# Attention feeding a two-layer FFN on one core: new costs in the planner, and x, softmax sums and gated activations that stay in PSUM

## The chip, the cores and the metric

The program runs on one core of a Trainium2 chip, in one launch. The metric is the device time of that launch in microseconds (us). Three runs of the kernel before took 990.47, 990.62 and 991.66 us; the median, 990.62 us, is the number to compare with. One more execution was recorded by the profiler. Its own device time was 991.34 us, and the stretch from its first to its last instruction, the span, was 989.3 us.

## The reference

For 8 batches of 8 heads (576 positions, 64 columns per head) two attentions are added: one over q, k and v averaged in groups of 4 positions, its output repeated 4 times, and one over a band of 7 positions around each position. The sum, seen as 4608 tokens of 512 columns, goes through two matrix products with a gate between them.

```python
q_d = q.reshape(B, H, Sd, 4, D).mean(axis=3)          # also k_d, v_d
out_d = softmax_attention(q_d, k_d, v_d)              # scale 1/sqrt(64)
out_up = np.repeat(out_d, 4, axis=2)
mask = np.abs(pos[:, None] - pos[None, :]) < 4
out_local = masked_softmax_attention(q, k, v, mask)
x = (out_up + out_local)  # -> [4608, 512]

h = x @ w_in                                          # [4608, 2048]
g = where(h >= 1, h, where(h <= -1, 0, (h + 1)**2 / 4))
return g @ w_out                                      # [4608, 512]
```

All inputs are float32, and q and k are drawn eight times larger than v.

## The kernel before

**Products.** TensorE multiplies in a reduced format (fp32r), so the big products are made from three: each matrix is split into a high part and a low part, and high times high, high times low and low times high are summed in PSUM. That is why x exists as `xh` and `xl`, the gate's output as `gh` and `gl`, and each weight block as two halves.

**The FFN.** The tokens are cut into chunks of 512, 256 and then ten of 384. For each chunk and each of 16 blocks of 128 hidden columns, `mm1` makes h in one PSUM bank with 12 matmuls (L647), four engine steps gate it (ScalarE relu and square at L659 and L660, VectorE minimum at L661, ScalarE cast to `gh` at L663, GpSimd subtraction to `gl` at L668), and `mm2` adds the block's part of the output into up to four PSUM banks (L687). Two banks take turns for h. The weights come as raw 64-bit words and are converted on the chip in chunk 0 (`convert`: two ScalarE steps at L608 and L610, VectorE at L613 and L615, ScalarE at L620, VectorE at L623); after that they stay in SBUF.

**Attention.** It works on pairs of heads, four pairs to a batch, 32 in all. A pair passes these steps: VectorE sums q and k over groups of 4 (`qd`, `kd`, L340 and L344); TensorE makes the band scores in ten windows (L358, L370) and the pooled scores (L395); VectorE and ScalarE make maxima, exponentials and sums (L418 to L472); TensorE transposes both sets of weights (L488, L504), ScalarE copies them out (`al` L494, `ap` L512); GpSimd adds v over groups of 4 (`vh` L478, `vd` L480); TensorE multiplies with v (L527) and with vd (L545); ScalarE scales the pooled result (`xd` L555), VectorE adds both (`x` L563), ScalarE casts it to `xh` (L577) and GpSimd subtracts to get `xl` (L582). Batch 0 is needed before chunk 0 can start; later pairs are worked in between the FFN's matmuls, each a chunk ahead. x lives in a ring that holds two batches.

**What sets the order.** Every step is first recorded as an operation with an engine, a cost, what it needs, the buffers it holds, and a key. `Plan.run` then simulates five engines with these costs, always takes the operation that can start earliest (within a window of 0.15 us the lowest key wins), and so fixes each engine's order and each buffer's place. The program is then written out in that order. Each engine works its list strictly in order on the chip, so an operation that waits holds up everything behind it on its engine, wherever the chip's times differ from the plan's. Loads and stores are all issued from SyncE's queue, in the planned order too. PSUM has eight banks; a pair's PSUM tiles take two neighbouring ones, during batch 0 any of four such places, later only banks 0 and 1 (with bank 2 for part of the scores).

Of the kernel before, what the change touches and what calls it, by code (L numbers as in the profile page):

```python
# [17 lines left out]
P = 128  # L18
# [56 lines left out]
class Op:  # L75
    __slots__ = ("eng", "cost", "fn", "deps", "bufs", "key", "n", "left", "next", "start", "end", "nbytes", "name", "shared")


class Plan:
# [4 lines left out]
    DMA_RATE = 370e3  # L84
    DMA_LATENCY = 2.0
    WINDOW = 0.15
    BACKLOG = 4.0

    def __init__(self):
        self.ops = []  # L90
        self.pools = {}
# [4 lines left out]
    def op(self, eng, cost, fn, deps=(), bufs=(), key=0.0, nbytes=0, name="", shared=False):  # L96
        o = Op()
        o.eng, o.cost, o.fn, o.key, o.n = eng, cost, fn, key, len(self.ops)
        o.deps = list({id(d): d for d in deps if d is not None}.values())
        o.bufs, o.nbytes, o.name, o.shared = list(bufs), nbytes, name, shared  # L100
        for b in o.bufs:
            b.users += 1
        self.ops.append(o)
        return o

    def run(self):
# [9 lines left out]
        avail = {}  # L116
        busy = set()
        users = {}
        dma_free = 0.0
        pool_busy = []  # L120
        for o in self.ops:
            if not o.left:
                ready[o.eng].append(o)

        def settle(o):
            t = 0.0
            for d in o.deps:
                e = d.end
                if d.eng != o.eng:
                    e += self.PE_LATENCY if d.eng == "PE" else self.LATENCY  # L130
                t = max(t, e)
            return t
# [11 lines left out]
        based = {}  # L144
        done = []
        total = len(self.ops)
        while len(done) < total:
            best = None
            for e in engines:
                cands = []  # L150
                for o in ready[e]:
                    t = based.get(o.n)
                    if t is None:
                        t = based[o.n] = settle(o)
                    ok = True
                    for b in o.bufs:
                        if b.units is None:
                            got = pick(b)
                            if got is None:
                                ok = False  # L160
                                break
                            t = max(t, got[0] + self.LATENCY)
                    if ok:
                        if e == "SP":
                            t = max(t, dma_free - self.BACKLOG)
                        cands.append((max(t, free[e]), o))
                if not cands:
                    continue
                t0 = min(c[0] for c in cands)
# [595 lines left out]
```

## Time and profile before

| | before |
|---|---|
| median of 3 runs | 990.62 us (990.47 to 991.66) |
| profiled execution, its own time | 991.34 us |
| its span | 989.3 us |
| TensorE busy | 964.3 us, 97% of the span |
| VectorE busy | 431.8 us, 44% |
| ScalarE busy | 487.4 us, 49% |
| GpSimd busy | 340.1 us, 34% |
| first matmul of the FFN starts | 49.99 us |

In the profile PE is TensorE's matmuls, PEld its weight loads, DVE VectorE, ACT ScalarE, POOL GpSimd, and SPq SyncE's queue, which issues the loads and stores. Times in a trace are us from the span's start, a duration in a group's row is ns. A row of a timeline has the start, the duration, the engine, the line, the operation, the tiles (written<-read) with their shapes, how many were merged, and in brackets how long the engine had been idle before and what ended that wait. Consecutive instructions on one engine overlap a little: a row's duration runs to the acknowledged end, and the next one may start some 0.08 us earlier.

### The profile page before, as it was taken

How to read it: one execution, taken by the hardware profiler on the slowest of the kernel's cores; microseconds unless marked ns; L12 is line 12 of the kernel's file. 1: busy time of each engine (PE TensorE's matmuls, PEld its weight loads, DVE VectorE, ACT ScalarE, POOL GpSimd, SP SyncE). 2: the span in 40 equal slices, each digit the busy share in tenths (PEclk: the TensorE clock that was granted, in tenths of full speed). 3: DMA queues.
4: the chain of work that ended last, by engine and by line, in shares of the span. 5: the costliest groups of instructions: out<-in, count | busy, mean ns of one | idle time of the engine just before them, and what ended most of it. 6: DMA issues, size and time to landing. Idle time of an engine off the chain costs nothing.

```text
span 989.3 us, 18499 instructions
## 1 busy us (share of the span) xinstructions
PE 964.3 (97%) x7620; PEld 835.6 (84%) x7620; DVE 431.8 (44%) x704; ACT 487.4 (49%) x1063; POOL 340.1 (34%) x320
## 2 busy tenths in 40 slices
PE   6699999999999999999999999999999999999998
PEld 5477778988888889988888888998888888999997
DVE  7799994135644441135444461114454543111110
ACT  2788786454545444335445454435444554433433
POOL 3323333234333442223343433222443334222222
PEclk9689999999999999999999999999999999999999
DMA  9981112022112220002122220001221210000000
GB/s 273 366 327 50 51 50 69 1 66 79 51 51 82 61 65 33 0 25 82 50 76 70 74 62 27 32 1 56 76 74 50 82 51 15 32 1 1 33 1 32
DMA packets 26532, 66.24 MB, mean 67 GB/s; under 512 B 3152, under 2 KB 3152, under 8 KB 26448
## 3 DMA queue, kind: packets, MB, share of 16 engines
q1 hardware_dynamic: 26448, 65.06, 19.9%
q8 instruction: 60, 0.98, 0.4%
q14 instruction: 24, 0.20, 0.1%
HBM read 55.61 MB, written 9.44 MB: 66 GB/s over the span
## 4 chain that ended last, share of the span: by engine, by line
PE 88%; DVE 7%; DMA 3%; ACT 2%; issue 1%; SPq 0%; ACTq 0%; DVEq 0%
PE ps L687 39%; PE ps L647 38%; PE ps L370 2%; PE ps L527 2%; PE ps L504 2%; PE ps L488 2%; PE ps L545 2%; PE ps L395 2%; DMA vp<-vp 1%; DMA raw_i<-w_in 1%; DVE m L615 1%; ACT sp L450 1%; DVE mxp L445 1%; DVE sl L469 1%; DVE sums L460 1%
## 5 line engine op out<-in xcount | busy, mean ns | idle before, releaser
L647 PE MATMUL ps<-xh,w_i 128*128 128x384 f32 (+2 forms) x1536 | 395.8, 340 | 0.6 <-DVE x L563 0.6
L668 POOL TENSOR_TENSOR gl<-u,gh 128x384 fp32r<-128x384 f32 (+2 forms) x192 | 197.2, 1027 | 523.8 <-ACT gh L663 373.7
L687 PE MATMUL ps<-w_o,gh 128*128 128x512 f32 x1152 | 368.8, 401 | 0.0
L647 PEld LDWEIGHTS ps<-xh,w_i 128*128 128x128 f32 x1536 | 277.1, 189 | 22.7 <-issue 4.2
L661 DVE SCALAR_TENSOR_TENSOR u<-ps,u 128x384 f32<-128x384 f32 (+2 forms) x192 | 106.3, 554 | 434.3 <-ACT u L660 427.3
L647 PE MATMUL ps<-xl,w_i 128*128 128x384 f32 (+2 forms) x768 | 259.6, 338 | 0.0
L687 PEld LDWEIGHTS ps<-w_o,gh 128*128 128x128 f32 x1152 | 207.3, 188 | 40.2 <-issue 6.9
L687 PE MATMUL ps<-w_o,gl 128*128 128x512 f32 x576 | 226.5, 393 | 0.0
L659 ACT ACTIVATE u<-ps 128x384 f32<-128x384 f32 (+2 forms) x192 | 94.4, 491 | 229.3 <-PE ps L647 229.2
L663 ACT CAST gh<-u 128x384 fp32r<-128x384 f32 (+2 forms) x192 | 98.5, 513 | 107.0 <-DVE u L661 100.1
L647 PEld LDWEIGHTS ps<-xl,w_i 128*128 128x128 f32 x768 | 144.6, 188 | 3.0
L687 PEld LDWEIGHTS ps<-w_o,gl 128*128 128x128 f32 x576 | 108.1, 188 | 25.3
L660 ACT ACTIVATE u<-u 128x384 f32<-128x384 f32 (+2 forms) x192 | 100.8, 525 | 5.6
L450 ACT ACTIVATE sp<-ps,mxp 128x144 f32<-128x144 f32 x96 | 35.4, 377 | 73.4 <-DVE mxp L445 73.3
L478 POOL TENSOR_TENSOR vh<-vp 72x512 f32<-72x512 f32 x32 | 41.8, 1306 | 66.3 <-PE ps L527 34.6
L582 POOL TENSOR_TENSOR xl<-x,xh 128x576 fp32r<-128x576 f32 x32 | 46.3, 1446 | 24.2 <-ACT xh L577 15.7
L423 DVE TENSOR_TENSOR sl<-ps,band_sb 128x640 f32<-128x640 f32 x24 | 19.8, 825 | 54.7 <-PE ps L395 37.1
L563 DVE TENSOR_TENSOR x<-ps,xd 128x576 f32<-128x576 f32 x32 | 24.2, 756 | 35.6 <-ACT xd L555 34.7
L428 POOL TENSOR_TENSOR sl<-sl,mxl 128x640 f32<-128x640 f32 x24 | 30.3, 1261 | 26.1 <-DVE mxl L426 26.1
L504 PE MATMUL ps<-ident,sp 128*72 128x128 f32 x192 | 28.2, 286 | 8.6 <-DVE x L563 8.5
L504 PEld LDWEIGHTS ps<-ident,sp 128*72 128x72 f32 x192 | 21.9, 120 | 14.1 <-DVE x L563 8.7
L527 PEld LDWEIGHTS ps<-al,v 64*64 64x64 f32 x1280 | 22.9, 139 | 9.8 <-issue 4.9
(60 smaller groups left out, 756.3 us busy)
## 6 DMA issues: line engine op xcount, KB each, us to landing
v<-vw SPq DMA_DIRECT2D x32, 320.0 KB
vp<-vp SPq DMA_DIRECT2D x32, 288.0 KB
out<-osb SPq DMA_DIRECT2D x36, 256.0 KB
raw_i<-w_in SPq DMA_DIRECT2D x16, 512.0 KB
raw_o<-w_out SPq DMA_DIRECT2D x16, 512.0 KB
q<-qT SPq DMA_DIRECT2D x28, 288.0 KB
k<-kT SPq DMA_DIRECT2D x28, 288.0 KB
qf<-qT SPq DMA_DIRECT2D x4, 288.0 KB
```

Source lines behind the costliest of these rows:

```text
L450: nc.scalar.activation(spb.tile[:, i], sp_view()[:, i] if i < 2 else sp_other(), AF.Exp, bias=mxb.tile[:, i : i + 1], scale=scale, accum_o ...
L478: o_vh = op("POOL", 1.32, lambda: nc.gpsimd.tensor_tensor(vhb.tile, vpb.tile[:, :, 0:2, :], vpb.tile[:, :, 2:4, :], op=ALU.add), [l_vp, No ...
L504: nc.tensor.transpose(tp_v[:, kb, i, :], spb.tile[:, i, kb * KB : (kb + 1) * KB], ident if i < 2 else swapped,)
L527: nc.tensor.matmul(pl_v[hs, o : o + OUT_LEN[i]], vb.tile[rs, 2 * g + h, :], alb.tile[rs, g, c0 : c0 + OUT_LEN[i]], start=True, stop=True,)
L582: o_xl = op("POOL", 1.445, lambda: nc.gpsimd.tensor_tensor(xl[:, p, r0 : r0 + S], xb.tile, xh[:, p, r0 : r0 + S], op=ALU.subtract), [o_xh] ...
L647: nc.tensor.matmul(h, wi[:, wt, cc * P : (cc + 1) * P], xt[:, cc, ts], start=(i == 0), stop=(i == 3 * NCC - 1))
L659: o2 = op("ACT", 0.49 + e, lambda: nc.scalar.activation(u(), h(), AF.Relu, bias=0.5, scale=0.5), [o1], [hb, ub], key, name=f"relu {c},{f}")
L660: o3 = op("ACT", 0.52 + e, lambda: nc.scalar.activation(u(), u(), AF.Square), [o2], [ub], key, name=f"sq {c},{f}")
L661: o4 = op("DVE", 0.556 + e * 1.2, lambda: nc.vector.scalar_tensor_tensor(u(), h(), 1.0, u(), op0=ALU.max, op1=ALU.min), [o3], [hb, ub], ke ...
L663: o5 = op("ACT", 0.51 + e, lambda: nc.scalar.copy(ghb.tile[:, :n], u()), [o4], [ub, ghb], key, name=f"gh {c},{f}")
L668: o6 = op("POOL", 1.06 + e * 2.5, lambda: nc.gpsimd.tensor_tensor(glb.tile[:, :n], u(), ghb.tile[:, :n], op=ALU.subtract), [o5], [ub, ghb, ...
L687: nc.tensor.matmul(o, g.tile[:, ts], wb.tile[:, wt, :], start=f == 0 and i == 0, stop=f == NFC - 1 and i == 2)
```

## The change

1. **The planner's model.** A load occupies SyncE for 0.45 us and has its own cost in us in place of bytes over a common rate (0.76 for q or k, 1.15 for vp, 0.95 for v, 1.31 for a weight block, 0.7 for a store); the backlog allowed is 6 us instead of 4. Operations that use the SBUF port that GpSimd and VectorE share are marked (`port=True`): all GpSimd operations and the VectorE steps of the weights' conversion. The planner never lets two of them overlap, where it stretched some of them before. An operation may have a second way of being done on another engine, and the planner takes it where it starts soon enough. Its constants K are new.
2. **Softmax.** The maxima of the pooled scores and all softmax sums and their reciprocals are kept in the PSUM bank of the pooled scores, in place of small SBUF tiles.
3. **x.** VectorE adds x in place in PSUM; ScalarE casts `xh` from there, and VectorE, not GpSimd, subtracts `xl` from there, for all 32 pairs (`xp0` equals `xp1`). The PSUM tile is held until `xl` is made.
4. **The gate.** In all chunks but chunk 0 the minimum is written in place into h's PSUM bank, `gh` is cast from there and `gl` is subtracted by VectorE. h's bank is held until `gl` is made. In chunk 0 this part is as before, on GpSimd.
5. **Second ways.** Of the operations that may go to another engine, only the sums of q and k of two of batch 0's pairs do: GpSimd makes them, in two additions each. The others stay where they were.

The core of the diff:

```diff
 class Plan:
-    DMA_RATE = 370e3
     DMA_LATENCY = 2.0
+    ISSUE = 0.45
+    BACKLOG = 6.0
...
+                    if way[3]:
+                        t = max(t, port_free)
...
-                if o.shared:
-                    for a, z in pool_busy[-4:]:
-                        end += max(0.0, min(end, z) - max(t, a)) * 0.7
-                if o.eng == "POOL":
-                    pool_busy.append((t, end))
-                free[o.eng] = o.end = end
+                free[o.eng] = o.end = t + cost
+                if port:
+                    port_free = o.end
...
+        def sums_of(dst, src):
+            src = src.rearrange("p (s f) -> p s f", f=FACTOR)
+            half = hab.tile.rearrange("p (s f) -> p s f", f=2)
+            nc.gpsimd.tensor_tensor(half, src[:, :, 0:2], src[:, :, 2:4], op=ALU.add)
+            nc.gpsimd.tensor_tensor(dst, half[:, :, 0], half[:, :, 1], op=ALU.add)
...
+        def mx_ps():
+            return spp.tile[:, 0, 2 * SD : 2 * SD + NQB]
+
+        def sums():
+            return spp.tile[:, 0, 2 * SD + 4 : 2 * SD + 4 + NB + NQB]
...
-                    accum_out=sums_w.tile[:, NB + i : NB + i + 1],
+                    accum_out=sums()[:, NB + i : NB + i + 1],
...
-            nc.vector.tensor_scalar_add(sums_w.tile, sums_w.tile, 1e-9)
-            nc.vector.reciprocal(parts_b.tile, sums_w.tile)
+            nc.vector.tensor_scalar_add(sums(), sums(), 1e-9)
+            nc.vector.reciprocal(sums(), sums())
...
-            slf(), slf(), parts_b.tile[:, 0:NB].unsqueeze(2).broadcast_to([P, NB, WIN]), op=ALU.mult),
+            slf(), slf(), sums()[:, 0:NB].unsqueeze(2).broadcast_to([P, NB, WIN]), op=ALU.mult),
...
-                xb.tile.rearrange("p (s f) -> p s f", f=FACTOR),
-                pl_v.rearrange("p (s f) -> p s f", f=FACTOR),
+                xs().rearrange("p (s f) -> p s f", f=FACTOR),
+                pl_s().rearrange("p (s f) -> p s f", f=FACTOR),
...
-            o_xl = op("POOL", 1.445, lambda: nc.gpsimd.tensor_tensor(xl[:, p, r0 : r0 + S], xb.tile, xh[:, p, r0 : r0 + S], op=ALU.subtract),
-                      [o_xh], [xb], kk[10], name=name + "xl")
+            o_xl = op("DVE", 0.755, lambda: nc.vector.tensor_tensor(xl[:, p, r0 : r0 + S], xs(), xh[:, p, r0 : r0 + S], op=ALU.subtract),
+                      [o_xh], [xheld], kk[10], name=name + "xl")
...
-        l = op("SP", 0, lambda: nc.sync.dma_start(wb.tile, src[f].rearrange("p (n t) -> p n t", t=2)), late if f >= 12 else (lq if f >= 8 else (lv_ops if f >= 4 else ())), [wb],
-               kc - K["wld"], nbytes=524e3, name=f"lw{kind}{f}")
+        l = op("SP", 1.31, lambda: nc.sync.dma_start(wb.tile, src[f].rearrange("p (n t) -> p n t", t=2)), late if f >= 12 else (lq if f >= 8 else (lv_ops if f >= 4 else ())), [wb],
+               kc - K["wld"], name=f"lw{kind}{f}")
...
+        on_pool = c == 0 and f in GL_POOL(K)
+        g = u if on_pool else h
+        held = ub if on_pool else hb
...
-            o6 = op("POOL", 1.06 + e * 2.5, lambda: nc.gpsimd.tensor_tensor(glb.tile[:, :n], u(), ghb.tile[:, :n], op=ALU.subtract),
-                    [o5], [ub, ghb, glb], key, name=f"gl {c},{f}")
+            o6 = op("DVE", 0.556 + e * 1.2, lambda: nc.vector.tensor_tensor(glb.tile[:, :n], g(), ghb.tile[:, :n], op=ALU.subtract),
+                    [o5], [held, ghb, glb], key, name=f"gl {c},{f}")
...
-K = dict(t0=40.0, conv=6.5, p0=6.5, p1=7.7, p1d=18.0, p2=-15.0, p2d=14.0, early=8, dk=2.3, ld0=70.0, lv0=7.5, ld=30.0,
-         clead=10.0, cio=11.9, wld=-35.0, lead=9.1, xlv=0, glv=0)
+K = dict(t0=10.0, conv=6.5, p0=6.3, p1=5.1, p1d=17.1, p2=-15.0, p2d=14.0, early=8, dk=3.4, ld0=100.0, lv0=0.0, ld=40.0,
+         clead=9.0, cio=9.0, wld=-130.0, lead=11.0, hv=60.0, vv=18.0, qp=-5.0, av=20.0, rv=10.0, gp0=0, gp1=16, xp0=8, xp1=8)
```

Three places show what this does to the order. The names are those of the tiles, with their numbers in the program; lines of the changed kernel are some 15 to 30 higher for the same step.

On ScalarE, in batch 0, around the first weight block `raw_i`, before (L512 copies `ap`, L608 and L610 are the conversion's first steps, L430 and L450 the exponentials, L555 `xd`, L494 `al`):

```order
L512 COPY ap_312<-ps 72x576
L608 ACTIVATE raw_i_256<-raw_i_256 128x512
L610 ACTIVATE raw_i_256<-raw_i_256 128x512
L608 ACTIVATE raw_i_270<-raw_i_270 128x512
L430 ACTIVATE sl_356<-sl_356 128x640
L555 ACTIVATE xd_377<-ps 128x144
L610 ACTIVATE raw_i_270<-raw_i_270 128x512
L450 ACTIVATE sp_384,sums_385<-ps,mxp_380 128x144 x3
```

and now (L519 is `ap`, L428 and L450 the exponentials, L623 and L625 the conversion, L499 `al`):

```order
L519 COPY ap_333<-ps 72x576
L428 ACTIVATE sl_323<-sl_323 128x640
L623 ACTIVATE raw_i_247<-raw_i_247 128x512
L428 ACTIVATE sl_338<-sl_338 128x640
L450 ACTIVATE sp_376,ps<-ps,mxp_348 128x144 x3
L499 COPY al_391<-ps 128x640
L625 ACTIVATE raw_i_247<-raw_i_247 128x512
L623 ACTIVATE raw_i_273<-raw_i_273 128x512
L625 ACTIVATE raw_i_273<-raw_i_273 128x512
L450 ACTIVATE sp_418,ps<-ps,mxp_406 128x144 x3
```

The first conversion now stands behind the third pair's exponential instead of ahead of it, and only one conversion step stands ahead of the fourth pair's softmax.

On VectorE, in batch 0, from the last softmax scaling of the fourth pair, before (L469 and L472 scale, L563 adds x, L613, L615 and L623 convert):

```order
L469 TENSOR_TENSOR sl_439<-sl_439,parts_486 128x640
L563 TENSOR_TENSOR x_516<-ps,xd_492 128x576
L472 TENSOR_TENSOR sp_467<-sp_467,parts_486 128x432
L623 TENSOR_TENSOR w_i_518<-m_471,w_i_518 128x512
L615 ISA m_482<-raw_i_270,m_482 128x1024
L613 TENSOR_SCALAR m_556<-raw_o_307 128x512
L563 TENSOR_TENSOR x_562<-ps,xd_552 128x576
```

and now (L468 and L471 scale, L577 adds x, L597 makes `xl`, L628, L630 and L639 convert):

```order
L468 TENSOR_TENSOR sl_338<-sl_338,ps 128x640
L577 TENSOR_TENSOR ps<-ps,xd_441 128x576
L471 TENSOR_TENSOR sp_418<-sp_418,ps 128x432
L630 ISA m_380<-raw_i_247,m_380 128x1024
L628 TENSOR_SCALAR m_479<-raw_i_273 128x512
L597 TENSOR_TENSOR xl<-ps,xh 128x576
L577 TENSOR_TENSOR ps<-ps,xd_487 128x576
L639 TENSOR_TENSOR w_i_490<-m_380,w_i_490 128x512
L630 ISA m_479<-raw_i_273,m_479 128x1024
L597 TENSOR_TENSOR xl<-ps,xh 128x576
```

The subtractions to `xl` have come into VectorE's list, and what scales or adds now reads one of its operands from PSUM.

On VectorE, in a later chunk of 384 tokens, where GpSimd made `gl` before, it now reads (L688 is the gate's minimum, L695 makes `gl`, L421, L424 and L442 belong to a pair of heads):

```order
L597 TENSOR_TENSOR xl<-ps,xh 128x576
L688 SCALAR_TENSOR_TENSOR ps<-ps,u_4803 128x384
L695 TENSOR_TENSOR gl_4834<-ps,gh_4820 128x384
L688 SCALAR_TENSOR_TENSOR ps<-ps,u_4842 128x384
L421 TENSOR_TENSOR sl_4884<-ps,band_sb 128x640
L424 TENSOR_REDUCE mxl_4891<-sl_4884 128x10
L695 TENSOR_TENSOR gl_4905<-ps,gh_4874 128x384
L442 TENSOR_REDUCE ps<-ps 128x1
```

Each block of a chunk now has two operations on VectorE, and the steps of a pair stand between them.

More of the change, by code (lines that the diff above doesn't have):

```diff
@@ L75, with __init__ @@
 class Op:
-    __slots__ = ("eng", "cost", "fn", "deps", "bufs", "key", "n", "left", "next", "start", "end", "nbytes", "name", "shared")
+    def __init__(self, n, ways, deps, bufs, key, name):
+        self.n, self.ways, self.deps, self.bufs, self.key, self.name = n, ways, deps, bufs, key, name
+        self.eng = self.fn = None
+        self.start = self.end = 0.0
 class Plan:
@@ L142, in pick @@
             return best
[L144 to L147, printed above, removed]
+        self.done = []
+        while len(self.done) < len(self.ops):
             best = None
@@ L150, in run @@
                 cands = []
[L151 to L155, printed above, removed]
+                for entry in ready[e]:
+                    t, o, way = entry
+                    t = max(t, free[e])
+                    if way is not o.ways[0] and t + way[4] > max(free[o.ways[0][0]], o.since):
+                        continue
+                    if way[3]:
+                        t = max(t, port_free)
+                    if e == "SP":
+                        t = max(t, dma_free - self.BACKLOG)
                     for b in o.bufs:
@@ L202, in run @@
-            ready[o.eng].remove(o)
-            done.append(o)
+                free[o.eng] = o.end = t + cost
+                if port:
+                    port_free = o.end
+            for w in o.ways:
+                ready[w[0]] = [x for x in ready[w[0]] if x[1] is not o]
+            self.done.append(o)
             for b in o.bufs:
@@ L213, in run @@
                 if not n.left:
-                    ready[n.eng].append(n)
-        self.order = sorted(done, key=lambda o: o.start)
-        self.done = done
-        return max(o.end for o in done)
+                    make_ready(n)
+        return max(o.end for o in self.done)
     def emit(self):
@@ L379, in attention @@
         slb = scratch("sl", [P, NG, 2, WIN], "sl")
-        o_sl = op("PE", 2.2 if first else 1.3 if early else 0.9, scores, [l_q, l_k, None if extra else before.get("tl")], [slp, qb, kb_], kk[1], name=name + "sl")
-        shares = b > 1
+        o_sl = op("PE", 2.2 if first else 1.3 if early else 0.9, scores, [l_q, l_k, None if extra else before.get("tp" if shares else "tl")], [slp, qb, kb_], kk[1], name=name + "sl")
         spp = psum([(2,)] if shares else pairs_of_banks)
@@ L483, in attention @@
+        o_vd = op("POOL", 2.05, halves, [l_vp, None if extra else before.get("al")], [vhb, vpb, vdb], kk[4], name=name + "vd", port=True,
+                  other=[("DVE", 1.23, whole, False, K["vv"])] if n < 8 else [])
         tlp = psum(pairs_of_banks)
```

197 lines of the change are left out of this document (100 added, 97 removed).

## The prediction, made before the changed kernel was run

> **What bounds the kernel now.** I read the page's busy times first, then the windows, to find where TensorE is not busy, then the timelines of that stretch.
>
> ```profile
> span 989.3 us, 18499 instructions
> PE 964.3 (97%) x7620; PEld 835.6 (84%) x7620; DVE 431.8 (44%) x704; ACT 487.4 (49%) x1063; POOL 340.1 (34%) x320
> 10.00:20.00 10.00, 6.81 (x153) 5.43 (x154) 9.80 (x19) 4.45 (x16) 4.43 (x4) 0.83 0.96 257
> 20.00:30.00 10.00, 1.08 (x11) 0.57 (x7) 5.20 (x7) 2.27 (x4) 4.17 (x4) 0.69 1.04 356
> 40.00:50.00 10.00, 6.17 (x114) 4.66 (x110) 9.97 (x13) 7.38 (x16) 5.50 (x4) 0.84 0.98 323
> 69.84:155.00 85.16, 83.53 (x681) 65.55 (x681) 82.13 (x122) 70.18 (x136) 32.87 (x24) 1.00 0.18 58
> 155.00:980.00 825.00, 823.93 (x6319) 725.11 (x6318) 290.38 (x489) 371.95 (x828) 283.94 (x271) 1.00 0.14 45
> ```
>
> The columns after the length are the busy times of PE, PEld, DVE, ACT and POOL, then TensorE's granted clock, the DMA share and GB/s. TensorE is idle for 989.3 - 964.3 = 25.0 us. The three windows before 50 us hold 3.19 + 8.92 + 3.83 = 15.9 of them; 69.84 to 155 holds 1.63, and the 825 us after it only 1.07. The number of matmuls does not change. So the time can fall only by what batch 0's attention loses before the FFN, and by 2.7 us behind that; behind 155 us there is almost only something to lose. The largest loss has a chain of owners:
>
> ```profile
> 27.66 0.67 ACT L608 ACTIVATE raw_i<-raw_i 128x512 f32<-128x512 f32 x1 [8.82 <-DMA raw_i<-w_in]
> 30.42 0.76 DVE L563 TENSOR_TENSOR x<-ps,xd 128x576 f32<-128x576 f32 x1 [5.15 <-ACT xd L555]
> 31.23 1.50 PE L504 MATMUL ps<-ident,sp 128*72 128x128 f32 x6 [8.47 <-DVE x L563]
> ```
>
> ScalarE reached the first weight conversion at 18.84 and stood there for 8.82 us, until the block had landed. The next exponential and xd stood behind it in its list, VectorE waited for xd, and TensorE for VectorE. The FFN's first blocks then came at:
>
> ```profile
> 49.99 1.22 PE L647 MATMUL ps<-xh,w_i 128*128 128x512 f32 x2 [0.55 <-DVE x L563]
> 54.70 0.39 PE L647 MATMUL ps<-xl,w_i 128*128 128x512 f32 x1
> 57.50 0.40 PE L647 MATMUL ps<-xl,w_i 128*128 128x512 f32 x1
> 69.45 0.39 PE L647 MATMUL ps<-xl,w_i 128*128 128x512 f32 x1
> ```
>
> These are the start of block 0's first product, its end (55.1), the end of block 1's (57.9), and the end of block 3's (69.84), by which time the second products of blocks 0 and 1 were done too. I measure the gain at this last point: four first products and two second ones.
>
> **When the first weight block lands.** SyncE keeps eight loads under way; it issues one when the eighth before it lands:
>
> ```profile
> 15.80 1.26 POOL L478 TENSOR_TENSOR vh<-vp 72x512 f32<-72x512 f32 x1 [1.55 <-DMA vp<-vp]
> 14.16 0.33 SPq L326 DMA_DIRECT2D k<-kT  x1
> 15.82 0.32 SPq L330 DMA_DIRECT2D vp<-vp  x1
> 17.19 1.77 SPq L604 DMA_DIRECT2D raw_i<-w_in  x2
> 25.06 0.33 SPq L604 DMA_DIRECT2D raw_i<-w_in  x1
> 26.60 0.33 SPq L604 DMA_DIRECT2D raw_o<-w_out  x1
> 27.66 0.33 SPq L604 DMA_DIRECT2D raw_i<-w_in  x1
> ```
>
> The issue at 15.82 meets the landing at 15.80, and the one at 27.66 the landing that ended ScalarE's wait. So the later three issues mark the landings of k, vp and raw_i of the earlier three: 25.06, 26.60, 27.66. The changed queue issues the weight block right after k, ahead of vp. The loads ahead are the same, so it lands 1.06 to 1.3 us after 25.06; I take **26.3**. That is 1.4 us earlier, not 9: the better planned pace does not make the block come early, it puts other work ahead of the wait.
>
> **What then lies between the landing and the FFN.** ScalarE and VectorE worked almost without a break from there:
>
> ```profile
> 27.66:50.64 22.98, 15.58 (x228) 12.01 (x229) 19.98 (x31) 19.64 (x45) 6.92 (x5) 0.65 0.99 366
> 12.09 1.59 DVE L469 TENSOR_TENSOR sl<-sl,parts 128x640 f32<-128x640 f32 x1
> 11.73 1.26 POOL L478 TENSOR_TENSOR vh<-vp 72x512 f32<-72x512 f32 x1 [10.38 <-DMA vp<-vp]
> 19.52 0.82 DVE L469 TENSOR_TENSOR sl<-sl,parts 128x640 f32<-128x640 f32 x1
> 41.87 1.90 DVE L623 TENSOR_TENSOR w_i<-m,w_i 128x512 fp32r<-128x512 f32 x1
> 25.32 0.72 POOL L480 TENSOR_TENSOR vd<-vh 72x256 f32<-72x256 f32 x1
> 45.82 0.68 DVE L623 TENSOR_TENSOR w_i<-m,w_i 128x512 fp32r<-128x512 f32 x1
> ```
>
> ScalarE spent 19.64 us busy from the first conversion to the last `xh` of batch 0. In the new order the same stretch of its list has one exponential less (it now precedes the wait) and one conversion step more: again 19.6, so not before 26.3 + 19.6 = 45.9. VectorE's operations are stretched where GpSimd reads SBUF: 1.59 beside `vh` against 0.82 alone, 1.90 against 0.68. With the sums in PSUM the softmax scalings have one SBUF operand and I let them run at 0.82; the conversions can still be caught. From its first conversion step (the landing plus 0.67, so 27.0) to the last `xl` its new list has 35 operations. Without stretching, each less 0.08 of overlap with the next, they are 8 of x and `xl` at 0.67 (0.76 at 30.42), 13 conversion steps at 0.36 to 0.61, 6.6 in all, two scalings at 0.75 and two at 0.52, and 10 small ones and reductions, 3.8: 18.3 us, so not before 45.3. Moving `xl` here costs VectorE four times 0.67; taking two pairs' sums of q and k to GpSimd gives back about the same.
>
> The two engines also wait for each other. I followed both lists and TensorE's between them: VectorE waits 0.7 for the third pair's exponentials, 0.9 for the fourth's (a new wait: the window sums now go into the bank that these exponentials read), and 0.6 for the last xd. So the last `xl` ends at about **47.5**. Block 0's first nine matmuls need only three pairs and run ahead; its last three end at 48.6 and block 1 at 51.3, with 2.7 a block as from 55.1 to 57.9. Block 2 needs block 0's bank: ScalarE's relu stands behind conversions, VectorE frees the bank at 52.5, block 2 ends at 55.2. A pair's scores (0.7), block 3 and two second products (2.8 each) end at 64.2, where before they ended at 69.84: 5.6 us. GpSimd's additions for pair 5 (1.26 + 0.72) fall among the conversions at 39 to 41 and can stretch one by up to 1.2, half of it on the path: 0.6. **Gain 5.0**, bounds 2.2 (VectorE and ScalarE idle as before, 3.3 us) and 7.5 (no waits between them).
>
> Small operations that now read and write PSUM have no row of exactly their kind. The large ones say that it costs nothing:
>
> ```profile
> L418 DVE TENSOR_REDUCE mxl<-ps 128x10 f32<-128x640 f32 x8 | 6.5, 814 | 0.0
> L426 DVE TENSOR_REDUCE mxl<-sl 128x10 f32<-128x640 f32 x24 | 19.6, 815 | 0.4
> ```
>
> The same reduction takes 814 ns from PSUM and 815 from SBUF. The Trainium skill speaks against the change here: Perfetto Trace Analysis, Optimizing Scalar/DVE Operations, gives VectorE an overhead per instruction of about 60 ns on SBUF and 125 on PSUM. By that, some seven operations for each of batch 0's pairs would cost 65 ns more, an estimate of 1.8 us of the gain; the rows above show no such difference, so the sum goes without it.
>
> **Chunk 0.** In 69.84 to 155 VectorE was busy 82.13 of 85.16 us, and TensorE idle 1.63. VectorE gets four `xl` more (3.0 us) but should lose stretching:
>
> ```profile
> L615 DVE CUSTOM_DVE_ANT_0 m<-raw_i,m 128x1024 uint16<-128x1024 uint16 x16 | 19.0, 1186 | 0.7 <-ACT raw_i L610 0.2
> 37.84 0.69 DVE L615 CUSTOM_DVE_ANT_0 m<-raw_i,m 128x1024 uint16<-128x1024 uint16 x1
> ```
>
> This step takes 1186 ns in the mean, against 0.69 for the one at 37.84, beside which GpSimd had nothing running; these 16 alone hold 8 us of stretching. I take a gain of **1.0**, between nothing and 1.63. ScalarE, 70.18 of 85.16, has room for a start 5 us earlier.
>
> **The later chunks.** Here `gl` moves to VectorE and h's bank is held through two more steps.
>
> ```profile
> 370.95 0.49 ACT L659 ACTIVATE u<-ps 128x384 f32<-128x384 f32 x1 [1.89 <-PE ps L647]
> 372.75 0.51 ACT L663 CAST gh<-u 128x384 fp32r<-128x384 f32 x1 [0.75 <-DVE u L661]
> 375.15 0.49 ACT L659 ACTIVATE u<-ps 128x384 f32<-128x384 f32 x1 [1.89 <-PE ps L647]
> 379.31 0.49 ACT L659 ACTIVATE u<-ps 128x384 f32<-128x384 f32 x1 [1.85 <-PE ps L647]
> L661 DVE SCALAR_TENSOR_TENSOR u<-ps,u 128x384 f32<-128x384 f32 x160 | 88.5, 553 | 396.7 <-ACT u L660 389.8 <-POOL gl L668 6.9
> 372.99 2.12 PE ps L647 x12
> ```
>
> The bank of the block at 370.95 is filled again by the one whose relu is at 379.31, whose first matmul starts 2.12 earlier (as at 372.99 for the one at 375.15), at 377.2. It becomes free at 372.75 + 0.51 + 0.55 (as L661) + 0.1 = 373.9. The slack is 3.3 us; the extra 160 x 0.55 = 88 us of VectorE lie beside matmuls (290.38 of 825 busy). Holding x's banks through `xh` and `xl` adds some 1.4 us (two steps like x's at 30.42) to each pair's hold, and 24 pairs share these 825 us. Bounds: a gain of 1.07 at most, a loss as in the rival below; I take a loss of **0.5**.
>
> **Sum.** 989.3 - 5.0 - 1.0 + 0.5 = 983.8 of span. The profiled execution took 2.04 more than its span and 0.72 more than the median: 983.8 + 2.04 - 0.72 = **985.1**. The likeliest case's own range is 983 to 987.5.
>
> **Rivals.** *More gain*: ScalarE and VectorE keep off each other's way, 7.5 with all of 1.63 and no loss: 981.5. For it: most of the waits I count are single steps. Against: VectorE at 9.97 of 10 from 40 to 50 us. *No change*: chunk 0 is VectorE's, and an earlier start only meets it sooner. If the stretching stays as it is, VectorE has 85.16 - 82.13 = 3.0 us of room and gets 3.0 more work, and the 5.0 are given back: 990.6. This is also the case in which the change does not do what it says, for the plan keeps GpSimd and VectorE apart only as long as the chip keeps the plan's times. *Slower*: h's bank. A pair's run on VectorE has stretches like this one:
>
> ```profile
> 205.24 0.81 DVE L460 TENSOR_REDUCE sums<-sl 128x10 f32<-128x640 f32 x1
> 208.35 0.98 DVE L472 TENSOR_TENSOR sp<-sp,parts 128x432 f32<-128x432 f32 x1
> ```
>
> Over four microseconds back to back, and now the gate's minimum and `gl` can both stand behind such pieces, with x and `xl` as well. It decides from 3.3 us of waiting in one block; at 0.4 us beyond it for each of the 24 pairs of later batches, 9.6 us: 994.7. Against it: the gate's steps stand between the pair's steps in the new list.
>
> **Chances.** Forecast 0.63, more gain 0.14, a smaller gain (987.5 to 988.6) 0.04, no change 0.11, slower 0.08. A measurement of this kernel tells about 0.2%, 2.0 us, from no change, so faster is 0.81, same 0.11, slower 0.08. The range, 981.2 to 990.0, leaves out the slower case, half of no change and part of more gain.
>
> **What would show it.** ScalarE's longest wait for a weight block shrinks from 8.8 to about 6 us, and it ends near 26.3; TensorE's first FFN matmul is 4 to 7 us earlier than 49.99; L468 and L471 no longer have 1.5 us rows; TensorE's idle time behind 155 us stays under 2 us. The forecast is wrong if the block lands much earlier or later, or if TensorE waits for L695 in the late chunks.

## The result, and the profile after

Four runs of the changed kernel took 999.11, 1000.87, 1000.98 and 1001.55 us, median 1000.92; the kernel before took 990.55 beside them. The ratio is 1.0101, with a 95% interval of 1.0084 to 1.0119: **slower by 10.4 us**, where 985.1 was forecast. The profiled execution is the one at 999.11, with a span of 997.3; the kernel before had 989.3. The two profiles thus differ by 8.0 us and the medians by 10.4: the profiled execution is the fastest of the four.

The same three windows of both kernels, before first (length, then busy time of PE, PEld, DVE, ACT and POOL, TensorE's granted clock, DMA share, GB/s):

```profile
0.00:65.00 65.00, 46.42 (x578) 36.87 (x579) 53.96 (x86) 38.94 (x89) 20.61 (x24) 0.79 0.95 328
65.00:165.00 100.00, 98.37 (x759) 78.17 (x759) 90.25 (x134) 79.77 (x155) 37.04 (x27) 1.00 0.21 72
165.00:975.00 810.00, 808.93 (x6239) 711.91 (x6239) 286.44 (x483) 363.92 (x812) 280.37 (x267) 1.00 0.14 46
```

```profile
0.00:65.00 65.00, 49.06 (x598) 38.56 (x599) 54.04 (x94) 42.30 (x95) 19.54 (x29) 0.87 0.99 338
65.00:165.00 100.00, 94.64 (x742) 74.86 (x741) 84.26 (x133) 77.52 (x151) 27.24 (x21) 1.00 0.20 65
165.00:975.00 810.00, 804.12 (x6198) 702.52 (x6197) 362.20 (x674) 358.44 (x806) 76.71 (x70) 1.00 0.15 46
```

TensorE idles less in the head (18.58 to 15.94 us), more in chunk 0 (1.63 to 5.36) and more behind it (1.07 to 5.88). VectorE is the second number to look at: in chunk 0 it is busy *less* than before, 84.26 against 90.25, and still TensorE waits more.

**The head** went as forecast. Rows of ScalarE and TensorE in the changed kernel:

```profile
24.90 0.65 ACT L623 ACTIVATE raw_i<-raw_i 128x512 f32<-128x512 f32 x1 [2.68 <-DMA raw_i<-w_in]
44.49 1.22 PE L663 MATMUL ps<-xh,w_i 128*128 128x512 f32 x2
52.73 0.73 PE L663 MATMUL ps<-xh,w_i 128*128 128x512 f32 x2 [1.33 <-DVE u L688]
64.79 0.40 PE L714 MATMUL ps<-w_o,gl 128*128 128x512 f32 x1
```

The block landed at 24.9, the FFN's first matmul started at 44.49, block 2 waited for its bank until 52.7, and the last row ends the second of two second products with four first products done: 65.2, against 69.84. That is 4.65 us of gain. From this point to the end the kernel before took 989.3 - 69.84 = 919.5, the changed one 997.3 - 65.2 = 932.1: **12.6 us were lost where 0.5 of further gain was forecast**. Chunk 0's first output copy divides them: it starts at 162.64, and at 162.69 in the kernel before. So 4.6 us were lost up to there and 8.0 behind it.

**Chunk 0.** The longest stop, on TensorE, then VectorE, then ScalarE:

```profile
120.24 0.39 PE L663 MATMUL ps<-xl,w_i 128*128 128x512 f32 x1
121.75 0.74 PE L493 MATMUL ps<-ident,sl 128*128 128x128 f32 x5 [1.12 <-DVE sp L471]
123.31 0.85 PE L511 MATMUL ps<-ident,sp 128*72 128x128 f32 x6 [0.82 <-ACT al L499]
124.86 0.50 PE L714 MATMUL ps<-w_o,gh 128*128 128x512 f32 x1 [0.46 <-DVE w_o L639]
```

```profile
116.37 0.32 DVE L442 TENSOR_REDUCE ps<-ps 128x1 f32<-128x144 f32 x1 [1.63 <-PE ps L393]
117.42 0.83 DVE L460 TENSOR_REDUCE ps<-sl 128x10 f32<-128x640 f32 x1
119.77 0.18 DVE L464 TENSOR_SCALAR ps<-ps 128x13 f32<-128x13 f32 x1 [0.87 <-ACT sp L450]
121.01 0.60 DVE L471 TENSOR_TENSOR sp<-sp,ps 128x432 f32<-128x432 f32 x1
```

```profile
118.34 0.38 ACT L450 ACTIVATE sp<-ps,mxp 128x144 f32<-128x144 f32 x1 [2.19 <-DVE ps L460]
118.82 0.38 ACT L450 ACTIVATE sp<-ps,mxp 128x144 f32<-128x144 f32 x1
```

TensorE's list has the pair's two transposes one behind the other, with the second product behind both. The window transposes L493 need a bank that is now held until L471 has read the sums in it; L511 needs the same banks again when ScalarE has copied `al`; and the second product's weights come only then. The pooled exponentials L450 waited for the window sums L460, which write other columns of the bank that L450 reads, and VectorE's next step waited for L450.

**The late loss.** TensorE's waits for L695, on PE and on its weight loads (us in total, times, longest us), and the first of three like places, at the start of a chunk:

```profile
PE ps L663 <- DVE gl L695: 4.8, 3, 1.6
PEld ps L663 <- DVE gl L695: 10.4, 16, 2.0
```

```profile
298.41 0.55 DVE L688 SCALAR_TENSOR_TENSOR ps<-ps,u 128x384 f32<-128x384 f32 x1
300.02 0.83 DVE L460 TENSOR_REDUCE ps<-sl 128x10 f32<-128x640 f32 x1 [1.05 <-ACT sp L450]
300.76 0.74 DVE L336 TENSOR_REDUCE qd<-q 128x144 f32<-128x576 f32 x1
301.42 0.55 DVE L695 TENSOR_TENSOR gl<-ps,gh 128x384 fp32r<-128x384 f32 x1
299.87 0.52 ACT L690 CAST gh<-ps 128x384 fp32r<-128x384 f32 x1
302.02 0.62 PE L663 MATMUL ps<-xh,w_i 128*128 128x384 f32 x2 [1.60 <-DVE gl L695]
```

The gate's minimum was done at 298.96. `gh` stood on ScalarE behind the three exponentials until 299.87; `gl` stood on VectorE behind the window sums, which waited 1.05 for the exponentials, and behind `qd`, until 301.42. Both hold h's bank, so the next first product starts at 302.02. TensorE loses 1.6 us here by the record, 2.0 by its weight loads, and again at 540.9 and 779.8. Of the 10.4 us of held weight loads these three places have 6, and chunk 1 most of the rest:

```profile
PEld ps L663 <- DVE gl L695: 3.8, 12, 0.3
```

This is the same view for 165 to 213 us: 12 of chunk 1's 16 blocks of 256 tokens have their weight loads held for 0.3 us each. PE counts as busy there, which is why its idle time shows nothing. About half of the 3.8 is lost time: from chunk 0's first output copy to the last one of chunk 1 the changed kernel takes 50.7 us, and 48.9 in the same order with h's bank free (e2 below); with the sums in SBUF it is 49.5 against 47.6 (e1 and e3).

### The profile page after: what moved, and what is told of

The parts are those of the page before. It is cut to its first block, busy times and chain, and to the rows that moved or that the text cites. A ratio compares the mean times of both kernels' runs of the same rounds, so it can differ in the third digit from the quotient of the medians.

```text
span 997.3 us, 18271 instructions
## 1 busy us (share of the span) xinstructions
PE 965.8 (97%) x7620; PEld 831.5 (83%) x7620; DVE 505.0 (51%) x908; ACT 485.3 (49%) x1063; POOL 123.5 (12%) x120
## 4 chain that ended last, share of the span: by engine, by line
PE 84%; DVE 8%; ACT 3%; DMA 2%; issue 1%; SPq 0%; ACTq 0%; DVEq 0%
PE ps L714 38%; PE ps L663 37%; PE ps L369 2%; PE ps L511 2%; PE ps L493 2%; PE ps L534 2%; PE ps L552 1%; ACT sp L450 1%; PE ps L393 1%; DMA raw_i<-w_in 1%; DVE m L630 1%; DVE ps L460 1%; DMA vp<-vp 1%; DVE m L628 1%; DVE xl L597 1%
## 5 line engine op out<-in xcount | busy, mean ns | idle before, releaser
L663 PEld LDWEIGHTS ps<-xh,w_i 128*128 128x128 f32 x1536 | 275.2, 188 | 31.7 <-DVE gl L695 10.4
L688 DVE SCALAR_TENSOR_TENSOR ps<-ps,u 128x384 f32<-128x384 f32 (+1 forms) x176 | 96.5, 548 | 257.9 <-ACT u L680 257.9
L695 DVE TENSOR_TENSOR gl<-ps,gh 128x384 fp32r<-128x384 f32 (+1 forms) x176 | 95.9, 545 | 107.6 <-PE ps L714 64.3
L690 ACT CAST gh<-ps 128x384 fp32r<-128x384 f32 (+1 forms) x176 | 83.1, 472 | 109.0 <-DVE ps L688 106.6
L450 ACT ACTIVATE sp<-ps,mxp 128x144 f32<-128x144 f32 x96 | 36.4, 380 | 28.2 <-DVE ps L460 14.1
L421 DVE TENSOR_TENSOR sl<-ps,band_sb 128x640 f32<-128x640 f32 x24 | 19.8, 825 | 55.4 <-PE ps L393 49.5
L428 ACT ACTIVATE sl<-sl 128x640 f32<-128x640 f32 x32 | 23.6, 737 | 37.0 <-POOL sl L426 28.4
L460 DVE TENSOR_REDUCE ps<-sl 128x10 f32<-128x640 f32 x32 | 26.4, 826 | 16.1 <-ACT sp L450 13.8
L511 PE MATMUL ps<-ident,sp 128*72 128x128 f32 x192 | 27.4, 281 | 5.8 <-ACT al L499 5.1
L692 POOL TENSOR_TENSOR gl<-u,gh 128x512 fp32r<-128x512 f32 x16 | 22.6, 1411 | 78.8 <-ACT gh L690 61.1
L592 ACT CAST xh<-ps 128x576 fp32r<-128x576 f32 x32 | 20.4, 639 | 22.2 <-DVE ps L577 22.1
```

What stands on the lines that cost most here:

```text
L450: nc.scalar.activation(spb.tile[:, i], sp_view()[:, i] if i < 2 else sp_other(), AF.Exp, bias=mxb.tile[:, i : i + 1], scale=scale, accum_o ...
L460: o_su = op("DVE", 0.825, lambda: nc.vector.tensor_reduce(sums()[:, 0:NB], slf(), axis=AX.X, op=ALU.add), [o_e, o_sp], [slb, spp], kk[4], ...
L511: nc.tensor.transpose(tp_v[:, kb, i, :], spb.tile[:, i, kb * KB : (kb + 1) * KB], ident if i < 2 else swapped,)
L663: nc.tensor.matmul(h, wi[:, wt, cc * P : (cc + 1) * P], xt[:, cc, ts], start=(i == 0), stop=(i == 3 * NCC - 1))
L688: o4 = op("DVE", 0.556 + e * 1.2, lambda: nc.vector.scalar_tensor_tensor(g(), h(), 1.0, u(), op0=ALU.max, op1=ALU.min), [o3], [hb, ub], ke ...
L690: o5 = op("ACT", 0.50 + e, lambda: nc.scalar.copy(ghb.tile[:, :n], g()), [o4], [held, ghb], key, name=f"gh {c},{f}")
```

## The experiments

Each changes the changed kernel, unless it says otherwise. "In the same order" means that every engine's list stays as it was, so that only the waits differ. TensorE's idle time is read from the windows as above. The column "tail" is the time from the start of chunk 0's first output copy to the end of the span; it contains what TensorE loses without being idle, and leaves out the head, which differs from one execution to the next.

| run | edit | idle 65 to 165 | idle 165 to 975 | tail | median, us | ratio to before (95%) |
|---|---|---|---|---|---|---|
| before | | 1.63 | 1.07 | 826.6 | 990.55 to 991.52 | 1 |
| after | | 5.36 | 5.88 | 834.7 | 1000.92 | 1.0084 to 1.0119 |
| e1 | sums in SBUF, same order | 4.20 | 1.37 | 827.9 | 991.64 | 0.9997 to 1.0016 |
| e2 | gate in `u`, same order | 5.58 | 1.09 | 827.1 | 992.87 | 1.0011 to 1.0032 |
| e3 | both, same order | 4.16 | 0.07 | 823.8 | 987.75 | 0.9950 to 0.9976 |
| e4 | `gl` on GpSimd from `u` | 5.57 | 1.36 | 827.9 | 995.55 | 1.0027 to 1.0064 |
| e5 | e3, planner told | 1.43 | 0.04 | 823.8 | 985.72 | 0.9920 to 0.9959 |
| e6 | e5 and p1 2.1 | 0.22 | 0.00 | 823.5 | 982.99 | 0.9904 to 0.9933 |
| e7 | kernel before, `gl` on VectorE from h's bank | 1.62 | 0.00 | 825.9 | 990.26 | 0.9979 to 1.0001 |
| e8 | e3, x in SBUF, same order | 4.37 | 0.00 | 823.3 | 985.24 | 0.9927 to 0.9958 |
| e9 | p1 2.1 alone | 0.65 | 6.15 | 835.2 | 997.37 | 1.0046 to 1.0080 |
| e10 | e6, sums in PSUM | 0.97 | 0.70 | 826.9 | 987.94 | 0.9950 to 0.9976 |
| e12 | e6, x in SBUF, same order | 0.22 | 0.00 | 823.2 | 981.65 | 0.9884 to 0.9930 |
| e13 | e6, gate in h's bank, planner told | 0.23 | 1.38 | 827.8 | 987.31 | 0.9947 to 0.9975 |
| e14 | e13 and p2 -17 | 0.23 | 0.00 | 824.3 | 983.50 | 0.9909 to 0.9960 |
| e15 | p1 2.1 and p2 -17 alone | 0.88 | 1.27 | 829.4 | 990.13 | 0.9983 to 1.0008 |

### Each bank by itself, in the same order (e1 to e3)

```diff
         def sums():                                  # e1, e3
-            return spp.tile[:, 0, 2 * SD + 4 : 2 * SD + 4 + NB + NQB]
+            return <SBUF tile [P, NB + NQB], four in turn>
...
-        g = u if on_pool else h                      # e2, e3
+        g = u
```

> The changed kernel with the 13 softmax sums and their reciprocals in SBUF tiles (four in turn) instead of in the bank of the pooled scores; every engine's list keeps the changed kernel's order. Theory A, the shared bank: the window sums (L460) and the pooled exponentials (L450) now exclude each other, which the planner does not know, and this is what takes TensorE's time in chunk 0 (idle 5.4 us between 90 and 150) and a part of the three late waits. Then L450's waits for L460 and L460's for L450 go, TensorE's idle time between 65 and 165 falls from 5.4 to about 2, the late ones by 0.5 to 1 each: 994 to 997. Rival B, the changed order itself is too tight in chunk 0: no more than 1 us less, 1000. Rival C, the port: the scalings L468 and L471 get two SBUF operands back and are stretched to 1.5 us where GpSimd runs, and the head loses 1 us or more: above 1000.

> The changed kernel with the gate's result in the SBUF tile u in all chunks, as in chunk 0: gh and gl read u, VectorE still computes gl in the later chunks, and h's bank is free behind L688. Every engine's list keeps the changed kernel's order. Theory A, h's bank: the three late waits of TensorE for L695 (about 2.3 us lost at each of 300, 540 and 779, with the queue behind them) are the bank being held through gh and gl; they go, and the time falls by 5 to 7: 994 to 996. Rival B, VectorE's added load: the second products wait for gl itself, and the time stays within 1.5 of 1000.9.

> Both edits, the sums in SBUF and the gate's result in SBUF, in the changed kernel's order. If both theories A hold, they add: 988 to 991, a little faster than the kernel before, with TensorE's idle time between 65 and 165 about 2 us and behind 165 below 2 us. If the loss lies in the order or in VectorE's load: 998 or more.

Measured 991.64, 992.87 and 987.75: the edits take 9.3, 8.1 and 13.2 us off. The three lie below the ranges given for theory A, by 2.4, 1.1 and 0.3 us, and the first two do not add. The late idle time shows why. With either bank freed it falls from 5.88 to 1.37 or 1.09, with both to 0.07. At the chunk starts the two holds are links of one chain, and taking out either one lets most of the other hide. TensorE's waits in e1 at those starts are 0.43 us each; one of them:

```profile
297.37 0.61 PE L663 MATMUL ps<-xh,w_i 128*128 128x384 f32 x2 [0.43 <-DVE gl L695]
```

In chunk 0 the banks explain little: 4.16 us stay with both freed. There the same place now reads

```profile
121.01 0.71 PE L493 MATMUL ps<-ident,sl 128*128 128x128 f32 x5
123.17 0.85 PE L511 MATMUL ps<-ident,sp 128*72 128x128 f32 x6 [1.44 <-ACT al L499]
118.02 0.38 ACT L450 ACTIVATE sp<-ps,mxp 128x144 f32<-128x144 f32 x1 [1.05 <-DVE mxp L444]
118.39 0.37 ACT L450 ACTIVATE sp<-ps,mxp 128x144 f32<-128x144 f32 x1
```

(e3). L493 no longer waits and the exponentials start as soon as their maxima are there, but what is won stops two instructions on, at `al`. So theory A of these expectations holds for the late loss and fails for chunk 0, and the rival named there, the order, is left. Rival C, the port, was real in size and did not matter: in chunk 0 of e1, VectorE's scaling L468 takes 1559 ns in the mean of three, against 822, and the kernel is still 9 us faster.

### Whose load it is (e4)

```diff
-        on_pool = c == 0 and f in GL_POOL(K)
+        on_pool = True
```

> The changed kernel with gl on GpSimd from u in all chunks, as the kernel before has it; the planner makes a new order for it. Theory A, h's bank: the late loss goes and chunk 0's stays: 994 to 996. Rival B, VectorE's load is the late loss: the same number, so this run against the one with gl on VectorE from u tells the bank from the load. If GpSimd's port costs VectorE more than the bank did: above 997.

995.55 fits theory A. But its late idle time, 1.36, is that of e2, 1.09, where VectorE still makes every `gl`. The 96 us of `gl` that moved to VectorE are therefore not what TensorE waits for; the bank is. On GpSimd `gl` is 2.7 us slower than on VectorE from `u`, in lists that are new; the tail has 0.8 of them, and where the rest goes was not followed up.

### The list of chunk 0 (e5, e6, e9)

```diff
-        held = ub if on_pool else hb
+        held = ub                                    # e5, e6: the planner frees h's bank behind L688
+        sumb = sbuf("sums", [P, NB + NQB], F32, "sums", range(4))   # and gives the sums buffers of their own
...
-K = dict(..., p1=5.1, ...)
+K = dict(..., p1=2.1, ...)                           # e6, and e9 without the rest
```

> The kernel of the run with both edits, with the planner told of them: the sums have SBUF buffers of their own, and h's bank ends its use at L688 (until now the lists were still those of the changed kernel). New lists come out. Theory D, the list: what chunk 0 still loses there (4.3 us between 70 and 130, against 1.8 in the kernel before) stands in the order, in which TensorE has a pair's transposes and a second product one behind the other with nothing between; a new list moves it: 985 to 987. Rival E, VectorE's work: chunk 0 is full whatever the list, 987.5 to 988.5.

> As the run before, with one number of the planner's table changed: batch 1's pairs are due 3 us earlier (p1 2.1 instead of 5.1). Theory D, the list: the pairs' steps then stand ahead of the conversions that TensorE waits for, chunk 0's lost time falls to 2 us or less, and the time is 983.5 to 985.5. Rival E, VectorE's work: the same work on the same engine, within 1 us of the run before.

> The changed kernel with the one number p1 2.1 instead of 5.1 and nothing else: sums, gate and x stay in their banks; the planner makes new lists. If the due time alone is chunk 0's loss, TensorE's idle time between 65 and 165 falls from 5.4 to 1 or less: 996. If the sums hold the bank of the pooled scores until the scalings are done, so that the window transposes L493 wait for L471 in any list (1.12 us at 121.75 in the changed kernel), part of it stays: 998 to 1000. The late waits stay as they are in both.

e5 with the planner told has 1.43 us of idle time in chunk 0 in place of 4.16, e6 with the due time of batch 1's pairs 3 us earlier 0.22. The times fit theory D (e6 lies 0.5 below the range given), but the intervals of e5 and e6 overlap, so the idle time is the better evidence. The sharpest of the three is e9: nothing of the change is undone, one number of its table differs, and chunk 0's idle time falls from 5.36 to 0.65. TensorE's list there:

```profile
122.44 0.74 PE L493 MATMUL ps<-ident,sl 128*128 128x128 f32 x5 [0.42 <-DVE sp L471]
122.94 0.71 PE L714 MATMUL ps<-w_o,gh 128*128 128x512 f32 x2
...
124.41 0.82 PE L511 MATMUL ps<-ident,sp 128*72 128x128 f32 x6
124.98 0.70 PE L714 MATMUL ps<-w_o,gh 128*128 128x512 f32 x2
```

The two transposes now have second products between them, which cover the copy of `al`. L493 still waits 0.42 for L471: that part is the sums' bank. Nearly all of chunk 0's idle time was the list. e9's time, 997.37, is 1.4 above the value that its expectation gives for this case, since the late loss (6.15) stays.

### h's bank in other lists (e7, e13, e14, and one run that could not show it)

```diff
-        o4 = ... scalar_tensor_tensor(u(), h(), ...)          # e7, the kernel before
+        o4 = ... scalar_tensor_tensor(g(), h(), ...)          # g is h from chunk 1 on, for gh and gl too
-        if c < K["glv"]:                                      # gl on VectorE
+        if c:
...
-K = dict(..., p2=-15.0, ...)                                  # e14, against e13
+K = dict(..., p2=-17.0, ...)
```

> The kernel before with one part of the change alone: from chunk 1 on the gate's result goes back into h's bank, and VectorE computes gl from it; old planner, old numbers, sums and x as they were. Theory A, the bank costs where it is held: TensorE's idle time behind 155 us rises from 1.07 to 3 or more at the chunks' starts, 993 or more. Rival F, the bank costs only together with the sums' bank, which delays gh and gl there: idle time as before, 990 to 991.5, or less, as GpSimd's port no longer stretches VectorE.

On balance the kernel before loses nothing by holding h's bank through `gh` and `gl`: 990.26 against 991.24 beside it, and the late idle time falls to 0.00. Rival F, that the bank costs only together with the sums' bank, fits. But this run also takes `gl` off GpSimd, so a cost of the bank and a gain from that can hide each other in it. To test that in the good list I kept e6's order and put the gate back into h's bank:

> The run with planned edits and p1 2.1, in the same order, with the gate's result back in h's bank from chunk 1 on (gh and gl read it there). If holding h's bank costs only together with the sums' bank, as the kernel before with this part alone has it (990.3 against 991.2): 982.5 to 984.5, TensorE idle below 1 us behind 165. If it costs at the three chunk starts by itself, as in the run with the sums in SBUF alone (three waits of 0.43 for L695): 985 to 987.

It took 986.63 with 1.58 us of late idle time, which answers nothing: this order gives the bank to the next first product behind L688, so `gh` and `gl` can read the next block's h there, and the program no longer computes the same thing. With the planner told (e13), and then with the pairs of the later batches due 2 us earlier (e14):

> The run with planned edits and p1 2.1 without its edit to the gate: from chunk 1 on gate, gh and gl stay in h's bank and the planner knows it, as in the changed kernel; the sums are in SBUF. If holding h's bank costs at the three chunk starts whenever a pair's softmax stands there: 985.5 to 988, TensorE idle 1.3 us or more behind 165, as with the sums in SBUF alone. If it costs only together with the sums' bank: 982.5 to 984.5, idle below 0.5.

> As the run before, with one number changed: the pairs of batches 2 to 7 are due 2 us earlier against their chunk (p2 -17 instead of -15), so that a pair's softmax no longer stands at the start of a chunk. If the place of the pair is what makes h's bank late, the late idle time falls below 0.5 us with the bank still held: 982.5 to 984.5. If the bank is late wherever the pair stands: as the run before, within 1 us.

e13 took 987.31 with 1.38 us of late idle time, so rival F falls: the bank costs by itself, with the sums in SBUF. e14 took 983.50 with 0.00, and the bank is still held until `gl` is made; the tail falls from 827.8 to 824.3. What decides is where a pair's softmax stands. In e13 it stands in the first block of a chunk, ahead of `gl` on VectorE; two us of due time move it away:

```profile
292.16 0.61 PE L663 MATMUL ps<-xh,w_i 128*128 128x384 f32 x2 [0.43 <-DVE gl L695]
291.56 0.55 DVE L695 TENSOR_TENSOR gl<-ps,gh 128x384 fp32r<-128x384 f32 x1
```

(e13; in e14 no first product behind 165 us waits for L695 on PE.) What stays wherever the bank is held is chunk 1: 3.3 us of held weight loads in e7 and e14, 3.8 in the changed kernel, and none in e6. What they cost in e14 is little: its tail is 0.8 us longer than that of e6.

### Sums and x by themselves in the good list (e10, e8, e12)

> The run with planned edits and p1 2.1 without its edit to the sums, which are in the pooled scores' bank again (the planner knows the bank's use as the changed kernel's does). Theory G, the sums' bank costs by itself: L493 waits for L471 in chunk 0 and the exponentials for the window sums: 985.5 to 988. Rival: with a good list and h's bank free it costs nothing: 982.5 to 984.

e10 is e6 without the edit to the sums. It takes 4.9 us more, so theory G holds: in a good list the sums' bank still costs. The tail has 3.4 of it (826.9 against 823.5), though TensorE's late idle time rises by 0.70 only. The rest I did not separate, and one profile of each cannot do it: e10's is the fastest of its five executions, e6's the slowest of its four.

```diff
         def xs():
-            return xb.tile if x_pool else pl_s()
+            return pl_s() if extra else <SBUF tile [P, S]>
```

> The run with both edits, in the same order, with x in SBUF instead of in place in its banks (all pairs but two of batch 0); VectorE still computes xl. If x's banks are held too long (TensorE waits 0.43 us for xl in chunk 0, and the next pair's scores use these banks): 986.5 or less. If holding them is free, as the prediction's 0.5 for the later chunks has it: 987 to 988.5. If xl, with two SBUF operands again, is stretched by GpSimd: 989 or more.

> The run with planned edits and p1 2.1, in the same order, with x in SBUF for all pairs but two of batch 0. If x's banks cost something where they are held (the run with both edits went from 987.75 to 985.24 by this alone, most of it ahead of 65 us in its one profile): 980 to 982. If that was the head's spread from one execution to the next: 982.5 to 983.5.

x in SBUF gave 985.24 against 987.75 (e8 against e3) and 981.65 against 982.99 (e12 against e6). Both point the same way and lie where the expectations put a cost of x's banks, but the intervals of both pairs overlap, and behind 65 us nothing tells the two apart: TensorE's idle time differs by 0.2 us at most, the tails by 0.5 at most. Whether x's banks cost 1 to 2.5 us in the head or nothing stays open. e12, 0.9884 to 0.9930 of the kernel before, is the fastest kernel here.

### The changed kernel with two other due times (e15)

```diff
-K = dict(..., p1=5.1, p1d=17.1, p2=-15.0, ...)
+K = dict(..., p1=2.1, p1d=17.1, p2=-17.0, ...)
```

> The changed kernel with two numbers of its table and nothing else: p1 2.1 instead of 5.1 and p2 -17 instead of -15; sums, gate and x stay in their banks. If the due times set what the held banks cost: chunk 0's idle time 65 to 165 stays near 0.65 as with p1 alone, the late idle time falls from 6.15 to 2 or less, and the time is 990 to 993. If the sums' bank costs at the chunk starts wherever the pair stands: 995 or more.

990.13: all of the change in place, sums, gate and x in their banks, and the 10.4 us are gone, with chunk 0's idle time at 0.88 and the late one at 1.27. Three waits of 0.22 for L695 are left of the three of 1.60. So it took both to make the change's loss, the held banks (e3) and two due times that were 3 and 2 us off. What the sums' bank still costs in good lists is read from e14, which differs from e15 by the place of the sums alone: 983.50 against 990.13, 6.6 us, with 5.1 of them in the tail; e10 against e6 gave 4.9. h's bank costs little there: e14 is 0.5 above e6, which has p2 -15.

## Why the prediction was wrong

**What held.** The head. The bank of block 2 came free at 52.7 for 52.5. TensorE's first FFN matmul started at 44.49, 5.5 earlier than 49.99. The gain was 4.65 for 5.0, but partly by luck. The block landed at 24.90 for 26.3, after a wait of ScalarE of 2.68 us where about 6 was forecast, and the stretch from there to the end of the last `xl` (47.75 for 47.5) took 22.9 us instead of 21.2: two errors that cancel. In e2, which has the same lists in the head, the block landed at 26.52, close to the forecast, and the gain was 2.6. TensorE's granted clock before 65 us was 0.87 against 0.79 as well, and its share was not separated. No 1.5 us rows of L468 and L471 are left:

```profile
L468 DVE TENSOR_TENSOR sl<-sl,ps 128x640 f32<-128x640 f32 x32 | 26.1, 815 | 0.6
L471 DVE TENSOR_TENSOR sp<-sp,ps 128x432 f32<-128x432 f32 x32 | 19.0, 595 | 0.0
L465 DVE RECIPROCAL ps<-ps 128x13 f32<-128x13 f32 x32 | 8.0, 251 | 1.1
L450 ACT ACTIVATE sp<-ps,mxp 128x144 f32<-128x144 f32 x96 | 36.4, 380 | 28.2 <-DVE ps L460 14.1 <-DVE mxp L444 11.6
L460 DVE TENSOR_REDUCE ps<-sl 128x10 f32<-128x640 f32 x32 | 26.4, 826 | 16.1 <-ACT sp L450 13.8 <-ACT sl L428 1.8
```

That small operations in PSUM cost next to nothing was right too: the reciprocal takes 251 ns there and 240 in the kernel before from SBUF. The 65 ns more that the Trainium skill's Perfetto Trace Analysis, Optimizing Scalar/DVE Operations, would give each are not in these rows. But that the head's gain owes something to the unstretched scalings is not shown: e1, with the sums in SBUF, has the stretch back and reaches the same point of the head at 64.7.

**The term "chunk 0, gain 1.0" failed** (measured: a loss of 4.6 us up to chunk 0's first output copy, with 3.7 us more idle time, so that the head's gain is given back by then). Its mechanism was half right. VectorE's stretching did shrink, from 81.97 to 75.51 us of work between 70 and 155. The step that failed was reading chunk 0's bound from VectorE's load, and the order only from the head. TensorE lost its time on the places of single instructions in its list, where a pair's transposes stood with nothing between them; I did not follow TensorE's list through chunk 0. The *no change* rival has the head's gain given back in chunk 0 too, but because VectorE is full, which it was not.

**The term "later chunks, loss 0.5" failed**: the tail grew by 8.0 us. The step that failed was the slack of h's bank. The mechanism is that of the *slower* rival, h's bank held through `gh` and `gl`, and TensorE waiting for L695, which the prediction also named as a sign of being wrong. I gave it 0.08 because the slack of a block was 3.3 us. That block was one from the middle of a chunk. At the start of a chunk the pair's softmax stood between the gate's steps, `gh` came 0.9 and `gl` 2.5 us after the minimum was done, and the slack was gone. Chunk 1's blocks have 256 tokens instead of 384; I measured no slack there, and 12 of 16 had none. The price was 3 places of 2 us and about 1.8 in chunk 1 (50.7 against 48.9), not 24 of 0.4. The sentence against the rival, that the gate's steps stand between the pair's in the new list, was the very thing that made them late. The bound on the other side failed as well: I took TensorE's 1.07 us of idle time for all that could be won here, but with both banks free (e3) the tail is 2.8 us shorter than in the kernel before, with only 1.0 less idle time: idle time does not count what TensorE loses while the record has it busy.

**The sums' bank had no term behind the head.** I found the wait of the exponentials for the window sums once, as 0.9 us of the fourth pair, and did not carry it to the 28 pairs of the later batches. The two groups above have it: 14.1 us of ScalarE's waits and 13.8 of VectorE's, of which the kernel before has none:

```profile
L450 ACT ACTIVATE sp<-ps,mxp 128x144 f32<-128x144 f32 x96 | 35.4, 377 | 73.4 <-DVE mxp L445 73.3
L460 DVE TENSOR_REDUCE sums<-sl 128x10 f32<-128x640 f32 x32 | 26.1, 817 | 9.8 <-ACT sl L430 9.6
```

These are idle times of two engines, not time lost: ScalarE waits less ahead of L450 in all, 28.2 against 73.4. The price is what freeing the bank gave, 4.9 us (e10 against e6) to 6.6 (e15 against e14), and 9.3 in the changed kernel's own order (e1). The Trainium skill's PSUM page (PSUM — Partial Sum Buffer, PSUM bank collisions raise a hardware error) states that two engines must not be in the same quarter of the partitions of one bank at once, whether or not their columns differ, and gives as the simple rule to guard PSUM by bank and not by address. The trace agrees as far as it goes: L450 and L460 touch different columns of one bank, on all 128 partitions, and each waits for the other; no run here lets them collide. The three exponentials also stand 0.48 us apart (118.34, 118.82) instead of 0.37 (e3: 118.02, 118.39), each starting only when the row that writes the sum of the one before into that bank has ended (118.78 for the first); in e3 the next one starts before that row's end. The planner has none of this: it plans the sums and the exponentials side by side, and the exponentials at 1.22 us.

## What to carry to other kernels

Moving a small tile into a PSUM bank that another engine reads lengthened single operations here by 20 ns at most (a 128x288 reduction took 467 ns, from 447), but it made the two engines take turns and held the bank until the tile's last reader was done; count both for every user of the bank. When a buffer is held longer, measure its slack at the places where the work around it changes (the start of a chunk, the short chunk, the first block behind a foreign step), not at a typical block. Where a planner fixes the order, try its due times before you judge the change: two numbers moved by 3 and 2 us were worth as much here as the whole loss.

## What was not expected of the hardware

The head differs from one execution to the next by 2 us for the same instructions: with lists that are the same up to there, the point at 65.2 in the changed kernel lies at 67.2 in e2, whose first weight block landed 1.6 us later. A gain in a head that is bound by loads is thus known from one profile only to about 2 us; the profiled execution of the changed kernel was also the fastest of its four, by 1.8 us. One of VectorE's shortest operations lost the most by GpSimd's use of SBUF: the 3 element scaling of the maxima took 816 ns in the mean in the kernel before (908 for the 28 that ran beside a GpSimd operation, 169 for the other four), and takes 161 with its input in PSUM, where 21 of the 32 still run beside one. How much of this time was on TensorE's path was not measured.
